# Pacing the loads of the prologue to three in flight, and moving one step of w_in's second slice, in a fused retention + SiLU MLP kernel

## The chip, the cores and the metric

The kernel runs on one core of a Trainium2 chip. A core has a matrix engine (PE; its weight loads are shown apart as PEld), a vector engine (DVE), a scalar engine (ACT), GpSimd (POOL), and SyncE (SP), which here issues nearly all DMA transfers, in the order in which they stand in its queue. Each engine works through its own list in order, and waits on semaphores for the others. The metric is the device time of one execution in microseconds; the median over several executions counts.

## The reference

What is computed is a retention layer, written as a recurrence, whose output is the input of a two-matrix MLP with SiLU:

```
q, k, v: (B=4, H=8, S=768, D=64) float32
state = gamma_h * state + outer(k_t, v_t)          # per batch and head, for t = 0..767
y_t   = scale * (q_t @ state)
x     = y as (B*S = 3072, H*D = 512)
h     = x @ w_in          # w_in  (512, 2048), stored as float64
out   = (h * sigmoid(h)) @ w_out   # w_out (2048, 512), stored as float64
```

## The kernel before

The sequence is cut into 6 chunks of 128 positions; a chunk of one batch is a unit, so there are 24 units, numbered 4 * chunk + batch. For a unit, k, q and v (256 KB each) are loaded; k and q are turned over by PE into PSUM (tiles `kp`, `qp`) and copied out by ACT (`kt`, `qt`); DVE scales k by the decay (line 424); PE forms the scores and the state's increment (`sc`, lines 518 and 528); DVE masks the scores (`am`, line 536) and forms `mid` and `state`; PE forms `y` (line 576), which is split by ACT and DVE into three parts (`xt`). A product of the MLP takes `xt` of a whole chunk (512 rows) and one 128-column slice of w_in, also in three parts (`wi`), and is closed by ACT and DVE (`gk` or `g`).

w_in comes as float64. `load_w(i)` loads a slice as words in three transfers, one of 256 KB (line 193) and two of 128 KB (line 195). The generator `early_slice(i)` turns it into float32 and then splits it; each call `W(i)` runs one step of it. For slice 1, the eighth call copies the high part on ACT (line 126), the ninth and tenth form the two low parts on DVE (line 118); the earlier calls do the conversion (lines 212 to 231).

The first two chunks or so (units 0 to 8, the first steps of unit 9, and the first products of the MLP) are written out by hand, call by call, and for SP, DVE, ACT and POOL the order of the calls is the order of the queues; PE's order is written by hand throughout. In it `T`, or `TK` and `TQ`, turn k and q over, `K` scales k, `SC` forms scores, `A` does DVE's steps on them, `Q` scales q, `YS`, `Y0` and `YB` form y, `X` splits it, `PP` and `PH` are parts of MLP products, `CL` closes one. `load("q", 6)` issues the load of unit 6's q. Calls that only concern different engines can stand in either order without any effect.

All loads of units 0 to 5 and of slices 0 and 1 are issued at the start, one behind the other. Those from `load("k", 6)` on are written among the calls of units 3 to 8, far ahead of their use. In the queue, each transfer also waits on a semaphore of its own lane, of which there are eight used in turn (DMAHW0 to DMAHW7); a transfer that goes into a buffer waits for the buffer's last readers as well.

Of the kernel before, what the change touches and what calls it, by code (L numbers as in the profile page):

```python
# [35 lines left out]
def kernel(  # L36
# [28 lines left out]
    nc = tc.nc  # L65
    B, H, S, D = q.shape
    DM, DF = moe_w_in.shape
    C = 128
# [64 lines left out]
    def split_w(*of):  # L133
        steps = split_steps(*of)
        next(steps)
        yield
        list(steps)
# [15 lines left out]
    early, last = {}, []  # L153

    def load(name, n):
        if n >= len(units):
            return
        c, b = units[n]
        src = {"k": k, "q": q, "v": v}[name]
        if n == 4 * B and name == "k":  # L160
            t = conv.tile([128, H, D], FP32, tag="wl", name=f"kf_{n}")
            nc.sync.dma_start(out=t, in_=src[b, :, ds(c * C, C)].rearrange("h t d -> t h d"))
            kqv[name][n] = t
            return
        if n < EARLY:

            if n not in early:
                early[n] = wpool.tile([128, 3, H, D], FP32, tag=f"w{4 + n}", name=f"kqv_{n}")
            t = early[n][:, "kqv".index(name)]
        else:  # L170
            t = ld.tile([128, H, D], FP32, tag=f"{name}f", name=f"{name}f_{n}",
                        bufs=2 if name == "q" else 3)
        nc.sync.dma_start(out=t, in_=src[b, :, ds(c * C, C)].rearrange("h t d -> t h d"))  # L173
        kqv[name][n] = t

    staged = {}

    def load_w(i):
        if i >= 2 * NF:
            return
        if wide:
            t = stage.tile([128, 2 * DM], U32, tag="wf", name=f"wf_{i}")
            w_in, w_out, n = moe_w_in.bitcast(U32), moe_w_out.bitcast(U32), 256
        else:
            t = stage.tile([128, DM], FP32, tag="wf", name=f"wf_{i}")
            w_in, w_out, n = moe_w_in, moe_w_out, 128
        if i < NF:  # L190
            to = t.rearrange("p (i o f) -> o p i f", o=2, f=n)
            src = w_in[:, ts(i, n)].rearrange("(i o p) f -> o p i f", o=2, p=128)
            last[:] = [nc.sync.dma_start(out=to[0], in_=src[0]).ins]
            for j in range(2):
                nc.sync.dma_start(out=to[1, ts(j, D)], in_=src[1, ts(1 - j, D)])
        else:
            nc.sync.dma_start(out=t, in_=w_out[ts(i - NF, 128), :])
        staged[i] = t
# [35 lines left out]
    def convert_w(i):  # L234

        if patient[0]:
            waiting.append(i + W_AHEAD)
        elif i + W_AHEAD not in staged:
            load_w(i + W_AHEAD)
        out = []  # L240
        steps = convert_steps(i, out)
        for _ in range(6):
            next(steps, None)

        def rounded():
            list(steps)
            return out[0]

        return rounded

    def early_slice(i):

        out = []
        yield from convert_steps(i, out)
        yield
        steps = split_steps(i, out[0], "wi", w_sb, None)
        next(steps)
        yield from steps
# [44 lines left out]
    def begin_w():  # L303

        i = taken[0]
        taken[0] += 1
        split = split_w(i, convert_w(i)(), "wi", w_sb, True)
        next(split)
        half_split.append(split)
# [102 lines left out]
    def hold(done):  # L412

        i = nc.sync.nop().ins
        tc.add_manual_dep(i, done.name, mybir.DependencyInfo(
            mybir.DependencyClass.Sync, mybir.DependencyReason.DATA), reason="hold")
# [276 lines left out]
    def halves(m):  # L693
# [36 lines left out]
        for name in "kqv":  # L730
            for n in (m + 1, m + 2):
                if (n, name) not in apart and EARLY <= n <= LATER and n == (
                        m + 1 if name == "v" or n >= LATER else m + 2):
                    load(name, n)
# [144 lines left out]
    def A(n):  # L879
        next(asteps[n], None)  # L880
# [7 lines left out]
    def TQ(n):  # L888
        next(tsteps[n])
# [20 lines left out]
    def W(i, times=1):  # L910
        if i not in slices:
            slices[i] = early_slice(i)
        for _ in range(times):
            next(slices[i], None)

    def loads(n):
        for name in "kqv":
            load(name, n)
# [39 lines left out]
    def CL(f):  # L958
        next(closing[f], None)

    def KA(n):
        t = kqv["k"][n]
        for h in range(H):
            nc.scalar.activation(out=t[:, h, :], in_=t[:, h, :], func=AF.Copy,
                                 scale=gk[:, units[n][0], h : h + 1])


    load("k", 0)
    load("q", 0)
    load("v", 0)  # L970
    load_w(0)
    load("k", 1)
    load("q", 1)
# [5 lines left out]
    load("q", 3)  # L979
    load("v", 3)  # L980
    load_w(1)
    load("k", 4)
    load("q", 4)
# [83 lines left out]
    X(3)  # L1067
    TQ(4)
    W(1)
    load("k",6)  # L1070
    W(1)
    load_w(2)
# [9 lines left out]
    load("k",9)  # L1082
    PH(0,2,1)
    CL(0)
    W(1)
    load("v",7)
    A(4)
    load("k",8)
# [3 lines left out]
    Q(4)  # L1092
    A(4)
    K(5)
    W(1)
    CL(0)
    YS(4)
# [104 lines left out]
    Q(8)  # L1202
    load("q",11)
    taken[0] = 3
    begin_w()

    early_order.close()
# [9 lines left out]
    last = ([(c, f) for c in range(2) for f in range(NF - 4, NF)] +  # L1217
            [(2, f) for f in range(half, NF)])
# [84 lines left out]
    def apart_cols(t):  # L1303

        return t.rearrange("p (o n) -> p o n", o=2)

    def unwoven(t):

        return t.rearrange("p (n o) -> p o n", o=2)
# [8 lines left out]
    for c in range(NC):  # L1318
# [9 lines left out]
        for f in range(NF):  # L1328
# [4 lines left out]
            t = ready[n]  # L1333
            if f >= early_f:
                continue
            for b in range(B):
                gh, glo, gm = (t[:, i, ts(b, C)] for i in range(3))
                oa, ob = acc[b]
                for o, g, i in (oa, gh, 0), (oa, glo, 1), (ob, gm, 2):
                    nc.tensor.matmul(o, lhsT=g, rhs=woven(wo[f][:, i, :],  # L1340
                                                          (c, b) == (NC - 1, B - 1)),
                                     start=f == 0 and i != 1,
# [4 lines left out]
        if early_f < NF:  # L1347
# [3 lines left out]
                         for x in ("left", "right")]  # L1351
            nc.scalar.activation(out=apart_cols(halves_of[0]),
                                 in_=unwoven(acc[B - 1][0][:, left]), func=AF.Copy,
# [7 lines left out]
        for b, o, parts, cols in ends:  # L1361
            for f in range(early_f, NF):
                for i in parts:
# [3 lines left out]
                                     start=o is last_left and (f, i) == (early_f, 0),  # L1367
                                     stop=f == NF - 1 and i != 0,
                                     skip_group_check=cols != whole)
        for b in range(B):  # L1370
            oa, ob = acc[b]
            if c == NC - 1 and b == B - 1:
# [4 lines left out]
                for i, (x, cols, op) in enumerate(((last_left, left, ALU.add),  # L1377
                                                   (oa, right, ALU.subtract))):
                    nc.vector.scalar_tensor_tensor(
                        out=apart_cols(o[i]), in0=unwoven(x[:, cols]), scalar=ONE_E,  # L1380
# [44 lines left out]
```

## Time and profile before

| | |
|---|---|
| median of 3 executions | 587.9 us (587.0 to 588.2) |
| the profiled execution's own time | 586.36 us |
| its span, first to last instruction | 584.4 us |
| PE busy, share of the span | 576.4 us, 99% |
| DVE, ACT, POOL busy | 399.1, 321.7, 29.4 us |
| granted PE clock | 0.999 |
| DMA, mean over the span | 186 GB/s |

The views give times from the span's start. A row of the timeline has the start, the duration, engine, line, operation, out<-in, shape, how many instructions were merged, and in brackets the engine's idle time ahead of it and what ended that. "issue" stands for idle time in which the engine waited for nothing that the profile shows. SPq rows are SP's issuing of a transfer: the duration is that of the issue, not that of the transfer, whose time from issue to landing stands in the list of DMA issues. PE's ends are modelled, so that a row without idle time can still hide a short one. The 2 us between the span and the execution's own time lie outside of the instructions.

### The profile page before, as it was taken

The page shows a single profiled execution, that of the slowest core. Times are in us where ns is not written, and L with a number is a line of the kernel's source. Part 1 is how long each engine was busy: PE and PEld are TensorE (multiplying, and loading weights), DVE is VectorE, ACT ScalarE, POOL GpSimd, SP SyncE. Part 2 cuts the span into 40 slices and gives each one's busy share as a digit, 9 for nine tenths or more (in the row PEclk, how much of TensorE's full clock was granted, in tenths as well). Part 3 has the DMA queues.
Part 4 walks back from the last instruction along what each step waited for, and adds up shares of the span by engine and source line. Part 5 has one row for each costly group of instructions (what it writes and reads, how often), then busy time and mean ns, then how long its engine had stood idle before and what let it go on. Part 6 is the DMA issues. An engine that isn't in the chain of part 4 may idle for free.

```text
span 584.4 us, 13651 instructions
## 1 busy us (share of the span) xinstructions
PE 576.4 (99%) x5512; PEld 499.9 (86%) x5512; DVE 399.1 (68%) x678; ACT 321.7 (55%) x561; POOL 29.4 (5%) x84
## 2 busy tenths in 40 slices
PE   8999999999999999999999999999999999999997
PEld 6787888888888888888888888888888888888886
DVE  3898998678678876666799994736545563645632
ACT  7657766546356466545566675544544545545311
POOL 3000000100031211210000000000000000000000
PEclk9999999999999999999999999999999999999999
DMA  9998978986489899997589862523524443433301
GB/s 193 215 220 192 218 192 278 267 259 214 145 192 232 234 283 284 255 265 230 171 281 326 288 207 77 195 93 111 178 79 139 144 119 97 165 123 102 115 1 72
DMA packets 144334, 108.89 MB, mean 186 GB/s; under 512 B 101136, under 2 KB 109584, under 8 KB 144272
## 3 DMA queue, kind: packets, MB, share of 16 engines
q1 hardware_dynamic: 144128, 107.90, 66.0%
q8 instruction: 43, 0.70, 0.5%
q14 instruction: 19, 0.16, 0.1%
q10 hardware_dynamic: 144, 0.13, 0.1%
HBM read 66.06 MB, written 36.70 MB: 176 GB/s over the span
## 4 chain that ended last, share of the span: by engine, by line
PE 95%; SPq 2%; DVE 1%; DMA 1%; issue 1%; ACT 0%; DVEq 0%; POOL 0%; POOLq 0%; ACTq 0%
PE ha L757 28%; PE o L1340 21%; PE oa L1340 14%; PE hb L757 14%; PE ob L1340 7%; PE y L576 4%; PE sc L518 2%; PE sc L528 2%; SPq L173 1%; DMA kqv<-in_q_dram 1%; PE ha L928 1%; PE kp L486 1%; PE qp L486 0%; PE o L1364 0%; PE hb L928 0%
## 5 line engine op out<-in xcount | busy, mean ns | idle before, releaser
L757 PE MATMUL ha<-xt,wi 128*128 128x512 f32 x736 | 175.7, 382 | 0.0
L757 PEld LDWEIGHTS ha<-xt,wi 128*128 128x128 f32 x736 | 137.7, 189 | 20.0
L1340 PE MATMUL o<-wo,gs 128*128 128x512 f32 x564 | 137.2, 379 | 0.0
L1340 PEld LDWEIGHTS o<-wo,gs 128*128 128x128 f32 x564 | 106.5, 189 | 15.3 <-DVE o L1389 0.2
L852 DVE TENSOR_TENSOR gs<-gr,gs 128x512 fp32r<-128x512 f32 x96 | 62.0, 684 | 83.0 <-ACT gs L850 83.0
L1340 PE MATMUL oa<-wo,gs 128*128 128x512 f32 x376 | 111.8, 379 | 0.0
L849 ACT ACTIVATE gr<-gr 128x512 f32<-128x512 f32 x96 | 59.7, 629 | 67.8 <-DMA gr<-gd 63.8
L757 PE MATMUL hb<-xt,wi 128*128 128x512 f32 x368 | 94.4, 379 | 0.0
L781 ACT ACTIVATE g<-ha 128x512 f32<-128x512 f32 x87 | 52.1, 599 | 76.5 <-PE ha L757 64.9
L787 DVE SCALAR_TENSOR_TENSOR g<-hb,g 128x512 f32<-128x512 f32 x87 | 59.7, 686 | 40.5 <-ACT g L781 33.6
L1340 PEld LDWEIGHTS oa<-wo,gs 128*128 128x128 f32 x376 | 71.1, 189 | 10.1
L757 PEld LDWEIGHTS hb<-xt,wi 128*128 128x128 f32 x368 | 69.6, 189 | 9.9
L850 ACT ACTIVATE gs<-gr 128x512 fp32r<-128x512 f32 x96 | 53.1, 621 | 38.7 <-PE ob L1340 30.4
L1340 PE MATMUL ob<-wo,gs 128*128 128x512 f32 x188 | 71.3, 379 | 0.0
L853 DVE SCALAR_TENSOR_TENSOR gs<-gs 128x512 fp32r<-128x512 f32 x96 | 61.9, 682 | 0.1
L1340 PEld LDWEIGHTS ob<-wo,gs 128*128 128x128 f32 x188 | 35.5, 189 | 5.1
L212 ACT ACTIVATE ca<-wf 128x512 f32<-128x512 f32 x32 | 27.1, 847 | 15.1 <-DVE cs L225 9.1
L225 DVE SCALAR_TENSOR_TENSOR cs<-ca,cs 128x512 uint32<-128x512 uint32 x32 | 22.1, 690 | 0.8
L536 DVE TENSOR_TENSOR am<-sc,decay 128x512 f32<-128x512 f32 x24 | 16.5, 686 | 8.8 <-PE sc L528 7.7
L576 PE MATMUL y<-qt,mid 64*64 64x64 f32 x376 | 20.0, 220 | 0.9 <-issue 0.9
L657 DVE SCALAR_TENSOR_TENSOR xt<-xt 128x512 fp32r<-128x512 f32 x28 | 19.6, 704 | 0.5
L1389 DVE TENSOR_TENSOR o<-o,o 128x512 f32<-128x512 f32 x10 | 6.6, 687 | 17.8 <-ACT o L1388 17.8
(137 smaller groups left out, 582.9 us busy)
## 6 DMA issues: line engine op xcount, KB each, us to landing
gr<-gd SPq DMA_DIRECT2D x96, 256.0 KB, 2.8
gd<-g SPq DMA_DIRECT2D x87, 256.0 KB, 3.8
wf<-in_moe_w_out_dram SPq DMA_DIRECT2D x16, 512.0 KB, 4.4
out_dram<-o SPq DMA_DIRECT2D x23, 256.0 KB, 2.4
wf<-in_moe_w_in_dram SPq DMA_DIRECT2D x16, 256.0 KB, 4.4
wf<-in_moe_w_in_dram SPq DMA_DIRECT2D x32, 128.0 KB, 4.2
kf<-in_k_dram SPq DMA_DIRECT2D x16, 256.0 KB, 4.6
qf<-in_q_dram SPq DMA_DIRECT2D x16, 256.0 KB, 4.4
```

Source lines behind the costliest of these rows:

```text
L212: top = nc.scalar.activation(out=a.bitcast(FP32), in_=hi.bitcast(FP32), func=AF.Abs, scale=2.0 ** -3).ins
L225: nc.vector.scalar_tensor_tensor(out=s, in0=a, scalar=3, in1=s, op0=ALU.logical_shift_left, op1=ALU.bitwise_xor)
L576: i = nc.tensor.matmul(to[ts(e, D), o, a, :], lhsT=lhsT, rhs=rhs, start=key not in started, stop=True, skip_group_check=True).ins
L657: nc.vector.scalar_tensor_tensor(out=x[2], in0=x[1].bitcast(FP32), scalar=-1.0 / EPS, in1=x[0].bitcast(FP32), op0=ALU.mult, op1=ALU.add)
L757: nc.tensor.matmul(hb if i == 2 else ha, lhsT=w_sb[f][:, i, ts(kk, 128)], rhs=woven(xt[c][:, i, kk, :]), start=kk == 0 and i != 1, stop=kk ...
L781: copied[:] = [nc.scalar.activation(out=to, in_=ha, func=AF.Copy, scale=scale * ONE_E).ins]
L787: taken_out[:] = [nc.vector.scalar_tensor_tensor(out=to, in0=hb, scalar=-scale, in1=to, op0=ALU.mult, op1=ALU.add).ins]
L849: nc.scalar.activation(out=g, in_=g, func=AF.Silu)
L850: nc.scalar.activation(out=t[:, 0, :], in_=g, func=AF.Copy, scale=HALF)
L852: nc.vector.tensor_tensor(out=t[:, 1, :], in0=g, in1=high, op=ALU.subtract)
L853: nc.vector.scalar_tensor_tensor(out=t[:, 2, :], in0=t[:, 1, :].bitcast(FP32), scalar=-1.0 / EPS, in1=high, op0=ALU.mult, op1=ALU.add)
L1340: nc.tensor.matmul(o, lhsT=g, rhs=woven(wo[f][:, i, :], (c, b) == (NC - 1, B - 1)), start=f == 0 and i != 1, stop=f == NF - 1 and i != 0 o ...
```

## The change

From unit 6's k on, up to the end of the part written by hand, each load of k, q, v and of w_in's slices waits until the third load ahead of it has landed: `hold` makes SP wait for that transfer's semaphore. Until then only the lane, eight transfers back, and the buffer were waited for. The stores are not paced, and the loads behind `pace[0] = 0` aren't either; slice 5 of w_in is the first of them. The second part of the change moves the eighth call `W(1)` from ahead of `load("v", 7)` to behind `K(5)`, next to the ninth.

```
+    flying, pace = [], [0]
+
+    def paced(start, **operands):
+        if pace[0] and len(flying) >= pace[0]:
+            hold(flying[-pace[0]])
+        flying.append(start(**operands).ins)
+        return flying[-1]
...
-        nc.sync.dma_start(out=t, in_=src[b, :, ds(c * C, C)].rearrange("h t d -> t h d"))
+        paced(nc.sync.dma_start, out=t, in_=src[b, :, ds(c * C, C)].rearrange("h t d -> t h d"))
...
-            last[:] = [nc.sync.dma_start(out=to[0], in_=src[0]).ins]
+            last[:] = [paced(nc.sync.dma_start, out=to[0], in_=src[0])]
             for j in range(2):
-                nc.sync.dma_start(out=to[1, ts(j, D)], in_=src[1, ts(1 - j, D)])
+                paced(nc.sync.dma_start, out=to[1, ts(j, D)], in_=src[1, ts(1 - j, D)])
...
     W(1)
+    pace[0] = 3
     load("k",6)
...
     CL(0)
-    W(1)
     load("v",7)
...
     K(5)
+    W(1)
     W(1)
     CL(0)
...
     taken[0] = 3
+    pace[0] = 0
     begin_w()
```

`hold`, which stood in the kernel before without a caller:

```
    def hold(done):
        i = nc.sync.nop().ins
        tc.add_manual_dep(i, done.name, mybir.DependencyInfo(
            mybir.DependencyClass.Sync, mybir.DependencyReason.DATA), reason="hold")
```

On SP, the loads from unit 6's k to unit 6's v stood thus before (kqv_6 holds unit 6's k, q and v; wf_2 is slice 2 of w_in; kqv_5's three loads stand just ahead, on lanes 5, 6 and 7):

```order
L173 DMA kqv_6_821<-in_k_dram 128x8x64 [waits DMAHW0_49]
L193 DMA wf_2_823<-in_moe_w_in_dram 128x2x256 [waits DMAHW1_49,DVE_49,Activation_49]
L195 DMA wf_2_823<-in_moe_w_in_dram 64x2x256 [waits DMAHW2_49]
L195 DMA wf_2_823<-in_moe_w_in_dram 64x2x256 [waits DMAHW3_49]
L173 DMA kqv_6_821<-in_q_dram 128x8x64 [waits DMAHW4_49]
L173 DMA kqv_7_828<-in_k_dram 128x8x64 [waits DMAHW5_49]
L173 DMA kqv_6_821<-in_v_dram 128x8x64 [waits DMAHW6_49]
```

and stand thus now (what was lines 173, 193 and 195 is line 181):

```order
L181 DMA kqv_6_821<-in_k_dram 128x8x64 [waits DMAHW5_49,DMAHW0_49]
L181 DMA wf_2_824<-in_moe_w_in_dram 128x2x256 [waits DVE_49,DMAHW1_49,DMAHW6_49,Activation_49]
L181 DMA wf_2_824<-in_moe_w_in_dram 64x2x256 [waits DMAHW7_49,DMAHW2_49]
L181 DMA wf_2_824<-in_moe_w_in_dram 64x2x256 [waits DMAHW0_49,DMAHW3_49]
L181 DMA kqv_6_821<-in_q_dram 128x8x64 [waits DMAHW1_49,DMAHW4_49]
L181 DMA kqv_7_833<-in_k_dram 128x8x64 [waits DMAHW2_49,DMAHW5_49]
L181 DMA kqv_6_821<-in_v_dram 128x8x64 [waits DMAHW3_49,DMAHW6_49]
```

The order is the same; each has one more wait, for the lane three places ahead. The same holds for the 19 loads behind these, up to unit 11's q.

On ACT, around the high part of slice 1 (`wi1`), the list before (kt and qt are copies of k and q turned over, of units 4, 5 and 6):

```order
L487 COPY qt_4_818<-qp_4_802 128x512 [waits PE_49]
L781 ACTIVATE gk_7_880<-ha_0_0_704 128x512 [waits DMAHW6_49,DMAHW5_49,PE_49]
L126 ACTIVATE wi1_882<-cs_1_758 128x512 [waits DVE_49]
L487 COPY kt_5_895<-kp_5_889 128x512 [waits PE_49]
L487 COPY qt_5_903<-qp_5_890 128x512 [waits PE_49]
L487 COPY kt_6_992<-kp_6_986 128x512 [waits PE_49,Activation_49]
```

and now:

```order
L493 COPY qt_4_818<-qp_4_802 128x512 [waits PE_49]
L787 ACTIVATE gk_7_889<-ha_0_0_704 128x512 [waits DMAHW6_49,DMAHW5_49,PE_49]
L493 COPY kt_5_904<-kp_5_898 128x512 [waits PE_49]
L493 COPY qt_5_912<-qp_5_899 128x512 [waits PE_49]
L126 ACTIVATE wi1_918<-cs_1_758 128x512 [waits DVE_49]
L493 COPY kt_6_1004<-kp_6_998 128x512 [waits PE_49,Activation_49]
```

One ACT instruction went behind two copies. DVE's list has the same instructions in the same order as before; the moved call is one of ACT. PE's list too is unchanged, but for a wait on ACT at the first product with slice 1.

## The prediction

> **What bounds the kernel now.** I read the page first, then a table of stretches, PE's waits and its timeline, and last the loads: when they are issued, how long they take, who uses them. The page and the stretches (length; then busy time and instructions of PE, PEld, DVE, ACT, POOL; clock; share of the DMA engines; GB/s):
>
> ```profile
> span 584.4 us, 13651 instructions
> PE 95%; SPq 2%; DVE 1%; DMA 1%; issue 1%; ACT 0%; DVEq 0%; POOL 0%; POOLq 0%; ACTq 0%
> ...
> 26.00:54.00 28.00, 26.66 (x670) 22.53 (x671) 25.39 (x46) 18.12 (x40) 0.36 (x4) 1.00 1.00 216
> 54.00:60.00 6.00, 6.00 (x150) 5.20 (x152) 4.76 (x10) 4.25 (x10) 0.09 (x1) 1.00 0.68 169
> 60.00:300.00 240.00, 240.00 (x2806) 208.59 (x2796) 187.43 (x319) 137.32 (x216) 23.61 (x34) 1.00 0.87 234
> ```
>
> The second row is the chain that ended last: it is PE for 95%. From 60 to 300 us PE is busy in 240.00 of 240.00 us, so whatever makes PE later or earlier by 60 us moves the end by as much. The change acts on 26 to 60 us alone. There PE lacks 28.00 - 26.66 = 1.34 us, DVE is the next with 25.39 of 28, and the DMA engines are full (1.00). What PE waited for there:
>
> ```profile
> PE y L576 <- issue: 0.9, 2, 0.6
> PE sc L518 <- issue: 0.3, 1, 0.3
> PE y L576 <- POOL token L407: 0.3, 1, 0.3
> PE y L576 <- DVE qt L429: 0.2, 1, 0.2
> ```
>
> The reader is to see that no load is among them: before, every paced load landed ahead of its use. (One of the two "issue" waits of the first row, of 0.6 us, began ahead of 26 us.) So the loads can't be made to matter less; they can only stay hidden, or come out. What else is to be had is the rest of these waits, 1.3 us in 26 to 54 us.
>
> **The loads, one by one.** Issues on SP, then the transfers' times from issue to landing, in the order: unit 6's q, its v, the last piece of slice 2, the last of slice 3, and unit 5's k:
>
> ```profile
> 23.07 0.88 SPq L173 DMA_DIRECT2D kqv<-in_k_dram  x1
> ...
> 26.16 0.82 SPq L173 DMA_DIRECT2D kqv<-in_k_dram  x1
> ...
> 29.02 0.61 SPq L195 DMA_DIRECT2D wf<-in_moe_w_in_dram  x1
> 29.67 0.60 SPq L173 DMA_DIRECT2D kqv<-in_q_dram  x1
> ...
> 31.48 2.22 SPq L173 DMA_DIRECT2D kqv<-in_v_dram  x1
> ...
> 47.03 0.60 SPq L195 DMA_DIRECT2D wf<-in_moe_w_in_dram  x1
> ```
>
> ```profile
> kqv<-in_q_dram SPq DMA_DIRECT2D x1, 256.0 KB, 5.5
> kqv<-in_v_dram SPq DMA_DIRECT2D x1, 256.0 KB, 5.6
> wf<-in_moe_w_in_dram SPq DMA_DIRECT2D x1, 128.0 KB, 5.4
> wf<-in_moe_w_in_dram SPq DMA_DIRECT2D x1, 128.0 KB, 5.4
> kqv<-in_k_dram SPq DMA_DIRECT2D x1, 256.0 KB, 4.4
> ```
>
> So they landed at 29.67 + 5.5 = 35.2 (q6), 31.48 + 5.6 = 37.1 (v6), 29.02 + 5.4 = 34.4 (slice 2), 47.03 + 5.4 = 52.4 (slice 3) and 23.07 + 4.4 = 27.5 (k5). Their first uses, on PE and ACT:
>
> ```profile
> 36.40 0.60 PE L486 MATMUL qp<-ident,kqv 128*128 128x128 f32 x4
> 38.81 0.69 PE L518 MATMUL sc<-kqv 64*64 64x64 f32 x32
> 36.21 0.76 ACT L212 ACTIVATE ca<-wf 128x512 f32<-128x512 f32 x1
> 54.78 0.89 ACT L212 ACTIVATE ca<-wf 128x512 f32<-128x512 f32 x1
> ```
>
> The margins are 1.2 us for q6, 1.7 for v6, 1.8 for slice 2 and 2.4 for slice 3. Those of the other paced loads that I looked up are larger.
>
> **The change, part by part.**
>
> *The start of the pacing.* Unit 6's k, issued at 26.16, now waits for unit 5's k, which landed at 27.5: 1.4 us later. This costs nothing, since the engines are full: unit 5's q and v still lie in front of it, and the transfers that it would have waited behind are done meanwhile.
>
> *The pace, 256 KB loads.* In this stretch the engines moved 216 GB/s, which is 262,144 B / 216,000 B per us = 1.21 us for a load. With three in flight a load takes at least the time that it takes with little else on the queue, which a load of q shows that is issued at 166.60:
>
> ```profile
> 166.60 0.40 SPq L173 DMA_DIRECT2D qf<-in_q_dram  x1
> ...
> qf<-in_q_dram SPq DMA_DIRECT2D x1, 256.0 KB, 3.0
> ```
>
> Three in 3.0 us is one in 1.0 us, under 1.21. The engines then remain the limit, the time from issue to landing settles at 3 x 1.21 = 3.6 us instead of 5.5, and the landings come as often as before. Cost 0. The other bound is the shortest time of a load in the full stretch, the 4.4 us of unit 5's k: three in 4.4 us is one in 1.47, 0.26 us later with each load. I take the first, as with three in flight the queue is between the two, and 3.6 follows from the engines' own rate.
>
> *The pace, slices of w_in.* Their three transfers count as three, though they hold 512 KB together, so that 2 x 1.21 = 2.43 us of engine time now fill a turn of at least 3.0 us. That is 0.6 us later after each of the slices 2, 3 and 4. The engines also lose time whenever one of them is held up by something else and the other 15 run out of their three loads; an instruction fetch (below) is 1.25 us on one engine. I estimate 0.3 us per slice for it, a quarter of a fetch, so 0.9 us together. Above, all six transfers at the pace of 4.4 us would be late by 6 x 0.26 = 1.6 us at v6.
>
> *What then is late.* With 0.9 us, q6 lands at 36.1, 0.3 us ahead of its use; v6 at 38.0, 0.8 ahead; slice 3 (two slices' worth, 1.8 us) at 54.2, 0.6 ahead. All stay hidden, by little. What is queued behind the waiting load on SP is loads only, up to 62.88, where the first store stands. After the last paced load, at 53.92, SP issues nothing up to 57.77 anyway, as slice 5 waits for its buffer, and this takes up the lag:
>
> ```profile
> 53.92 0.82 SPq L173 DMA_DIRECT2D qf<-in_q_dram  x1
> 57.77 0.37 SPq L193 DMA_DIRECT2D wf<-in_moe_w_in_dram  x1
> ...
> 62.88 1.03 SPq L631 DMA_DIRECT2D yd<-ys  x1
> ```
>
> Cost 0, and if q6 is late by up to 0.3 us more, PE has some of it to spare: at 38.81 it starts right behind DVE's scaled k.
>
> *The moved step.* ACT and DVE around it:
>
> ```profile
> 30.37 0.63 ACT L126 ACTIVATE wi<-cs 128x512 fp32r<-128x512 f32 x1 [1.24 <-DVE cs L231]
> 30.91 0.57 ACT L487 COPY kt<-kp 128x512 f32<-128x512 f32 x1
> 31.38 0.59 ACT L487 COPY qt<-qp 128x512 f32<-128x512 f32 x1
> 35.25 0.59 ACT L487 COPY kt<-kp 128x512 f32<-128x512 f32 x1 [3.28 <-PE kp L486]
> 32.72 0.68 DVE L118 CUSTOM_DVE_ANT_0 wi<-cs,wi 128x512 fp32r<-128x512 f32 x1
> ```
>
> The list shows that it is an ACT step that goes behind two copies, and DVE's order stays. The copies can start as soon as PE has turned k over, some 0.2 us earlier; PE's waits above name no ACT copy. The high part then comes third, at about 31.8 to 32.4, still ahead of DVE's 32.72, which is where DVE arrives by its own list. ACT was idle for 3.28 us behind it. Cost 0, covered by DVE's queue; without that cover it would be 0.3 to 0.5 us.
>
> *The fetches.* PE's "issue" waits lie inside of runs of small matmuls. Ahead of the first of them, in 29.7 to 31.0 us, the DMA engines carried a transfer of kind "instruction"; then the three waits, the middle one from the chain (start, length):
>
> ```profile
> q8 instruction: 1, 0.02, 6.0%
> ...
> 32.50 0.27 PE L576 MATMUL y<-qt,state 64*64 64x64 f32 x1 [0.31 <-issue]
> ...
> 46.34 0.14 issue
> ...
> 52.39 0.27 PE L518 MATMUL sc<-vf,kf 64*64 64x64 f32 x1 [0.32 <-issue]
> ```
>
> 6.0% of 16 engines in 1.3 us is 1.25 us on one engine, in the middle of the loads' packets. Fewer loads in flight could shorten the fetch; a gain is bounded by the waits, 0.31 + 0.14 + 0.32 = 0.8 us. I take 0.1 us of gain: the engines are as full as before. The Trainium skill (DMA: Bandwidth & Descriptors, Queues, rings and completion order) has each engine take turns between the queues packet by packet, by which the depth of the loads' queue would not matter to a fetch at all, and the sum would have 0 here.
>
> *The sum.* 0 (start) + 0 (256 KB loads) + 0 to 0.3 (slices, as long as hidden) + 0 (moved step) - 0.1 (fetches): +0.1 us on the profiled execution's 586.36. The median of the runs shown is 587.9, 1.5 us above that one, so I forecast 588.0. The Trainium skill (DMA: Bandwidth & Descriptors, Anatomy of one DMA) gives 2.0 us plus bytes over 436 GB/s, 2.6 us for 256 KB. By that estimate the slices would cost less than 0.2 us each, and no margin would come near zero; the row of 3.0 us speaks against so short a time.
>
> **The rivals.**
>
> *Three in flight are too few* (slower). For it: margins of 0.3 to 0.8 us are left by my own count, and the bound of 4.4 us breaks them. Then q6 is late by 35.2 + 4 x 0.26 + 0.9 - 36.4 = 0.7, v6 by 37.1 + 1.6 + 0.9 - 38.8 = 0.8, and slice 3, 18 transfers on, by 52.4 + 18 x 0.26 + 1.8 - 54.8 = 4.1 us, from which PE's own lateness is to be taken. It decides once a load takes more than 3 x 1.21 = 3.6 us with three in flight. Halfway to the bound I get 1.5 us, so 589.5; at the bound 592. Against it: the idle queue's 3.0.
>
> *The fetches get short* (faster). If a fetch no longer shares its engine with loads, all of the three waits go, 0.8 us: 587.1. From 32.50 on, DVE, not PE, sets the next start at 38.81, so that the first of the waits would return there. Against it stands the full share of the engines, and the rule above. The Trainium skill (Runtime: NRT & Kernel Launch, Instruction fetch mechanics) calls the crossing of a 16 KiB block mostly hidden; the rows of 0.31 and 0.32 us differ.
>
> *Nothing happens* because the lanes paced the loads anyway. At most eight were in flight by them; at 5.5 us and 1.21 us a load it was 4 to 5, so three is less. This rival has the time of the forecast and is counted with it.
>
> **How the numbers follow.** Chances: all loads stay hidden 0.62, too few in flight 0.27, short fetches 0.11. Executions before lie between 587.0 and 588.2, so 0.2% (1.2 us) is about what a measurement can tell from no change. The first case is within 0.2% but for scatter (0.54, and 0.04 on each side); the second is slower by more in 0.20 and within in 0.07; the third faster by more in 0.05, within in 0.06. Together: faster 0.09, within 0.67, slower 0.24. The range goes from 586.9 (the fetch case) to 590.0 (the second case somewhat past its halfway value); above it I leave 0.08, below it 0.08.
>
> **What would show it.** In the changed profile: the paced loads at 3.5 to 3.8 us from issue to landing, against 5.5; SP's issues short, its time going into waits on landings; PE's waits without a load among them, and still with "issue"; the ACT copies of unit 5 ahead of the high part; slices landing about 1 and 2 us later. I am wrong if PE's waits from 36 to 59 us name a transfer, ACT's idle time ahead of line 212 does, or if the "issue" waits are gone.

## The result, and the profile after

The changed kernel takes 590.56 us (median of 6 executions, 588.83 to 591.35), the kernel before 588.02 (6 executions, 587.00 to 588.23): a ratio of 1.0047, interval 1.0035 to 1.0060. It is slower by 2.5 us, and 590.56 lies above the forecast of 588.0 and above its range. The profiled execution of the changed kernel took 589.75 us, 3.4 more than that of before.

From the page of the changed kernel, its chain of waits, and from its table of stretches the same three as before (length; busy time and instructions of PE, PEld, DVE, ACT, POOL; clock; share of the DMA engines; GB/s):

```profile
span 587.8 us, 13675 instructions
PE 90%; DMA 7%; SPq 2%; ACT 0%; issue 0%; DVEq 0%; DVE 0%
```

```profile
26.00:54.00 28.00, 24.77 (x644) 20.86 (x646) 25.69 (x46) 16.67 (x34) 0.35 (x4) 1.00 0.78 177
54.00:60.00 6.00, 5.45 (x67) 4.42 (x56) 3.83 (x8) 4.38 (x11) 0.00 (x0) 1.00 0.67 168
60.00:300.00 240.00, 238.96 (x2899) 207.74 (x2900) 185.91 (x317) 136.01 (x216) 23.02 (x35) 1.00 0.89 235
```

In the chain, transfers went from 1% to 7% and PE from 95% to 90%; SP's issuing has 2% in both. From 26 to 54 us the DMA engines are busy for 0.78 of the time and move 177 GB/s, where they were full and moved 216. PE's missing time has grown from 1.34 to 3.23 us there, and past 60 us, where it had none, it lacks 1.04.

PE's waits from 26 to 70 us (engine, tile, line, what was waited for; us in total, times, longest), and behind them the same waits on PE's timeline:

```profile
PE kp L502 <- DMA qf<-in_q_dram: 1.4, 2, 1.0
PE sc L524 <- DMA kqv<-in_v_dram: 1.3, 1, 1.3
PE qp L492 <- DMA kqv<-in_q_dram: 0.7, 1, 0.7
PE sc L524 <- DMA vf<-in_v_dram: 0.5, 1, 0.5
PE y L582 <- issue: 0.3, 1, 0.3
...
PE kp L502 <- DMA kf<-in_k_dram: 0.2, 1, 0.2
```

```profile
37.34 0.63 PE L492 MATMUL qp<-ident,kqv 128*128 128x128 f32 x4 [0.67 <-DMA kqv<-in_q_dram]
...
40.95 0.69 PE L524 MATMUL sc<-kqv 64*64 64x64 f32 x32 [1.26 <-DMA kqv<-in_v_dram]
...
53.38 0.69 PE L524 MATMUL sc<-vf,kf 64*64 64x64 f32 x32 [0.50 <-DMA vf<-in_v_dram]
...
60.44 0.27 PE L502 MATMUL kp<-ident,qf 64*128 64x64 f32 x1 [1.00 <-DMA qf<-in_q_dram]
...
65.91 0.24 PE L502 MATMUL kp<-ident,kf 64*128 64x64 f32 x1 [0.19 <-DMA kf<-in_k_dram]
...
66.87 0.27 PE L502 MATMUL kp<-ident,qf 64*128 64x64 f32 x1 [0.41 <-DMA qf<-in_q_dram]
```

These are unit 6's q and v, unit 8's v, unit 10's q, and unit 11's k and q. The six waits are 0.67 + 1.26 + 0.50 + 1.00 + 0.19 + 0.41 = 4.0 us. Of the three "issue" waits of before, the first is still there with 0.3; those of 0.14 and 0.32 are gone. So 4.0 - 0.46 = 3.5 us, against the 3.4 between the two profiled executions: the loss is PE's waiting for late loads, all of it before 67 us.

ACT came late to slices 2 and 3 as well (line 212 of before is 218 now):

```profile
36.72 0.67 ACT L218 ACTIVATE ca<-wf 128x512 f32<-128x512 f32 x1 [0.29 <-DMA wf<-in_moe_w_in_dram]
...
57.51 0.88 ACT L218 ACTIVATE ca<-wf 128x512 f32<-128x512 f32 x1 [1.27 <-DMA wf<-in_moe_w_in_dram]
```

No wait of PE names ACT or the slices' tiles, so these two cost the kernel nothing directly.

The paced loads: SP's issues for unit 6's k, slice 2, unit 6's v, and units 10's and 11's q, and transfer times from issue to landing, first of unit 6's k and v alone, then medians over the k, q and v loads issued from 36 to 54 us:

```profile
27.80 0.37 SPq L181 DMA_DIRECT2D kqv<-in_k_dram  x1
29.00 4.14 SPq L181 DMA_DIRECT2D wf<-in_moe_w_in_dram  x3
...
36.68 0.37 SPq L181 DMA_DIRECT2D kqv<-in_v_dram  x1
...
56.84 0.37 SPq L181 DMA_DIRECT2D qf<-in_q_dram  x1
...
62.14 0.52 SPq L181 DMA_DIRECT2D qf<-in_q_dram  x1
```

```profile
kqv<-in_k_dram SPq DMA_DIRECT2D x1, 256.0 KB, 4.7
...
kqv<-in_v_dram SPq DMA_DIRECT2D x1, 256.0 KB, 4.1
...
kf<-in_k_dram SPq DMA_DIRECT2D x3, 256.0 KB, 4.4
kqv<-in_v_dram SPq DMA_DIRECT2D x2, 256.0 KB, 3.7
qf<-in_q_dram SPq DMA_DIRECT2D x2, 256.0 KB, 4.7
vf<-in_v_dram SPq DMA_DIRECT2D x2, 256.0 KB, 4.9
```

A load of 256 KB with three in flight takes about 4.4 us, not 3.6 (single ones 3.2 to 5.4); SP's issues are short, as its time goes into the new waits; and the last paced load, unit 11's q, is issued at 62.14, where it stood at 53.92.

The moved step went where the order said:

```profile
30.84 0.58 ACT L493 COPY kt<-kp 128x512 f32<-128x512 f32 x1 [1.61 <-PE kp L492]
31.32 0.59 ACT L493 COPY qt<-qp 128x512 f32<-128x512 f32 x1
31.80 0.64 ACT L126 ACTIVATE wi<-cs 128x512 fp32r<-128x512 f32 x1
```

DVE's low part follows at 32.82, against 32.72 before.

### The profile page after: what moved, and what is told of

The parts are those of the page before. It is cut to its first block, busy times and chain, and to the rows that moved or that the text cites. A ratio compares the mean times of both kernels' runs of the same rounds, so it can differ in the third digit from the quotient of the medians.

```text
span 587.8 us, 13675 instructions
## 1 busy us (share of the span) xinstructions
PE 575.3 (98%) x5512; PEld 499.0 (85%) x5512; DVE 400.0 (68%) x678; ACT 322.2 (55%) x561; POOL 28.5 (5%) x84
## 4 chain that ended last, share of the span: by engine, by line
PE 90%; DMA 7%; SPq 2%; ACT 0%; issue 0%; DVEq 0%; DVE 0%
PE ha L763 27%; PE o L1348 21%; PE oa L1348 14%; PE hb L763 13%; PE ob L1348 7%; PE y L582 4%; DMA qf<-in_q_dram 2%; SPq L181 2%; DMA wf<-in_moe_w_in_dram 1%; PE sc L524 1%; PE sc L534 1%; DMA kf<-in_k_dram 1%; DMA kqv<-in_q_dram 1%; DMA vf<-in_v_dram 1%; DMA kqv<-in_k_dram 1%; PE o L1372 0%
```

## The experiments

Every kernel is compared with the kernel before on the same chip. In most of them the lateness of loads is what tells. It is worked out thus, from rows as above: a load's landing (issue plus time to landing) less the landing of unit 5's k, one of the last three loads that nothing paces in any of them, and the one that unit 6's k waits for in the changed kernel, and this less the same for the kernel before. In the changed kernel, for instance, unit 6's k landed at 27.80 + 4.7 = 32.5, 4.8 behind unit 5's; before, 3.4 behind it; it is 1.4 late.

| late by, us | unit 6's k | 6's q | 9's v | 10's q | 11's q |
|---|---|---|---|---|---|
| the changed kernel | 1.4 | 1.9* | 5.4 | 6.2* | 8.0 |
| e2, pace alone | 1.3 | 2.7 | 4.6 | 5.1 | 7.2 |
| e3, four in flight | -0.1 | -0.6 | 3.2 | 3.8 | 6.0 |
| e4, a slice counts as one | 1.0 | 1.7 | 3.4 | 3.7 | 2.7 |
| e5, slices alone wait | -0.3 | 0.0 | 1.3 | 1.8 | 2.9 |
| e6, two in flight | 1.0 | 4.2 | 10.8 | 13.8 | 17.9 |
| e10, four, a slice as one | -0.3 | -0.5 | 0.4 | 0.2 | 0.2 |

(* the landing is missing in the records; it is taken from the start of PE's first matmul behind the wait.) Each row is one execution, and the scatter between executions is not small: in e1, which paces nothing, unit 9's v came 1.3 and unit 10's q 1.0 us later than in the profiled execution of before.

### e1: the moved step alone

```
-    pace[0] = 3
+    pace[0] = 0
     load("k",6)
```

> The eighth step of slice 1 is moved as in the change, and no load is paced. Theory L (late loads: with three in flight a load takes 4 to 5 us from issue to landing, and PE waits for it): same as before within 0.1%, PE's waits as before. Rival M (the moved ACT step delays DVE's low part and what follows): the whole +2.5 us is here, about 590.5, and DVE's row at line 118 starts later than 32.7 us.

586.41 against 586.61 us, ratio 1.0003 (0.9989 to 1.0017). The moved step costs nothing that can be told. PE waits for no load in e1. DVE's low part starts at 33.01, later than 32.7, but the high part is done at 32.6 (ACT) and the low part stands right behind DVE's scaling of k (32.40, 0.68 us long), so it is DVE's own queue that holds it. PE's waits with "issue" come to 1.8 us in this profile, more than before, so they are not the same from one execution to the next.

### e2: the pace alone

The eighth `W(1)` stands where it stood before:

```
     CL(0)
+    W(1)
     load("v",7)
...
     K(5)
     W(1)
-    W(1)
```

> The loads are paced as in the change, and the ACT step stays where it was. Theory L: the same as the whole change, ratio to before 1.0047 with its interval of about 0.001, and PE waits for unit 6's q, unit 6's v, unit 8's v and unit 10's q by name, 3 to 4 us together. Rival M: the time of before.

589.11 against 586.61 us, ratio 1.0046 (1.0030 to 1.0063): 2.5 us, so the whole loss comes with the pace. The stretch of 26 to 54 us and PE's waits up to 80 us of this kernel:

```profile
26.00:54.00 28.00, 25.79 (x670) 21.92 (x669) 25.96 (x47) 17.52 (x38) 0.35 (x4) 1.00 0.77 178
```

```profile
PE qp L492 <- DMA kqv<-in_q_dram: 1.4, 1, 1.4
PE kp L502 <- DMA qf<-in_q_dram: 1.0, 2, 0.8
PE kp L502 <- DMA kf<-in_k_dram: 0.6, 1, 0.6
```

Again 1.4 + 1.0 + 0.6 = 3.0 us of waits for loads, though spread otherwise: the longest is for unit 6's q, and no v is named. From unit 6's v at 39.60 to units 7's v, 9's q and 9's v, each three loads later, the landings stood at 44.16, 48.49 and 52.88: 4.4 us to a turn of three, from a landing to that of the load which waited for it. In the kernel before, the same four landed at 37.04, 41.41, 44.50 and 48.61, 3.9 to three loads, since the engines were not full all the time there either. The kernel before and e2 from 38 to 54 us:

```profile
38.00:54.00 16.00, 15.15 (x428) 12.61 (x422) 14.36 (x26) 11.03 (x28) 0.27 (x3) 1.00 0.91 207
```

```profile
38.00:54.00 16.00, 15.63 (x435) 13.19 (x434) 14.38 (x25) 10.92 (x26) 0.26 (x3) 1.00 0.76 177
```

So the pace costs (4.43 - 3.86) / 3 = 0.19 us for each 256 KB load here.

### e3: four in flight

```
-    pace[0] = 3
+    pace[0] = 4
```

> The change with four loads in flight instead of three, all else as in it. Theory L: if the turn is what counts, a load of about 4.5 us gives one landing in 1.13 us, which is the engines' own rate of 1.21, so the lateness is nearly gone: PE's waits on loads under 0.5 us together, ratio 1.000 to 1.001. Rival S (the extra wait on each load costs by itself, in SP's queue, whatever the depth): still more than 1.5 us above before.

587.06 against 586.61 us, ratio 1.0013 (1.0002 to 1.0024). Only unit 11's q was waited for, 1.1 us, which is more than the 0.5 expected. As four in flight take most of the loss away, the extra wait on each load is not what costs (rival S). Unit 6's k now waits for unit 4's v and goes out at 26.16, as before, and nothing is late up to unit 6's q; from there the lateness grows to 3.2 at unit 9's v and 6.0 at the end. It stayed below the margins until the very last load.

### e4: three in flight, a slice counts as one

The first piece waits, the last one is counted:

```
             for j in range(2):
-                paced(nc.sync.dma_start, out=to[1, ts(j, D)], in_=src[1, ts(1 - j, D)])
+                flying[-1] = nc.sync.dma_start(out=to[1, ts(j, D)], in_=src[1, ts(1 - j, D)]).ins
```

> Three in flight, but a slice of w_in counts as one load: only its first piece waits, and only its last piece is counted. If the slices' three-for-one counting is the main cost (the prediction put 0.6 us on each of three slices and 0 on the loads of 256 KB), PE's waits on loads fall from 4.0 us to under 1, ratio under 1.002. If it is the turn of the 256 KB loads, well over half of the loss stays, ratio 1.003 or more.

586.22 against 586.61 us, ratio 0.9995 (0.9984 to 1.0005). The loss is gone, though not all of the waits: those for loads come to 1.3 us, where under 1 was expected. PE's waits up to 80 us:

```profile
PE kp L502 <- DMA qf<-in_q_dram: 0.7, 1, 0.7
PE qp L492 <- DMA kqv<-in_q_dram: 0.6, 1, 0.6
PE sc L524 <- DVE kqv L430: 0.5, 1, 0.5
PE y L582 <- issue: 0.3, 1, 0.3
```

The wait for unit 6's q is as long as in the changed kernel, 0.6 against 0.7, so it is there without the counting too, but the way to it is another. SP's issue of unit 6's q, in the changed kernel and in e4:

```profile
33.27 0.53 SPq L181 DMA_DIRECT2D kqv<-in_q_dram  x1
```

```profile
31.74 0.54 SPq L181 DMA_DIRECT2D kqv<-in_q_dram  x1
```

In the changed kernel it goes out when slice 2's first piece has landed (33.2), and that piece was not late itself. In e4 it goes out 1.5 us earlier, takes 5.4 us behind unit 6's k and the three pieces of slice 2, and lands at 37.1, no earlier. The waits for v and for unit 11 are gone. At unit 11's q the lateness falls from 8.0 or 7.2 to 2.7 us, so three transfers instead of one cost (7.2 - 2.7) / 3 = 1.5 to (8.0 - 2.7) / 3 = 1.8 us for each of the three slices. What counting does to the engines is seen from 32 to 34 us, behind slice 2. The kernel before, the changed one, and e4 (the share adds up the times of packets, and can exceed 1):

```profile
32.00:34.00 2.00, 1.69 (x92) 1.52 (x96) 2.00 (x5) 0.00 (x0) 0.09 (x1) 1.00 1.32 220
```

```profile
32.00:34.00 2.00, 1.67 (x85) 1.49 (x88) 2.00 (x4) 0.44 (x1) 0.09 (x1) 1.00 0.15 46
```

```profile
32.00:34.00 2.00, 1.51 (x84) 1.38 (x88) 2.00 (x4) 0.44 (x1) 0.09 (x1) 1.00 0.74 199
```

In the changed kernel the three in flight there were unit 6's k and slice 2's first two pieces, with landings at 32.5, 33.2 and 33.6: so close together that the engines ran nearly empty (0.15) until the three loads issued behind them were under way.

### e5: only the slices wait

The transfers of k, q and v are counted, but wait for nothing:

```
-        paced(nc.sync.dma_start, out=t, in_=src[b, :, ds(c * C, C)].rearrange("h t d -> t h d"))
+        flying.append(nc.sync.dma_start(out=t, in_=src[b, :, ds(c * C, C)].rearrange("h t d -> t h d")).ins)
```

> Only the pieces of w_in's slices wait for the third load ahead; k, q and v are counted but go out without the wait. If the pieces' own waits were the cost (theory P), most of the 2.5 us is here. If the cost arises because the loads behind a slice spend their turns of three on its small pieces (theory T, by the run in which a slice counts as one), SP catches up behind each slice, q6 lands within 1 us of before, and the ratio is under 1.0015.

587.92 against 586.46 us, ratio 1.0017 (1.0005 to 1.0029), just beyond the expected 1.0015. In its profile no load is waited for; there are two longer waits with "issue" instead (0.82 at 42.30, 0.66 at 47.21), as in the profile of e1, whose median shows no loss. So the loss needs both kinds of waits: with those of the slices alone there is about a third of it (0.17% of 0.46%), and as no load is waited for, the profile does not show whether late loads cause even that; with those of k, q and v and one to a slice (e4) there is none that can be told.

### e6: two in flight

```
-    pace[0] = 3
+    pace[0] = 2
```

> The change with two in flight. Theory T: a turn, from one landing to that of the load which waited for it, was 4.4 us for k, q and v in the changed kernel and about 3.2 for pieces. With two in flight I expect some 4.0 us a turn for two, 2.0 per load, so that unit 11's q, 25 loads behind unit 6's k, lands near 32 + 25 x 1.9 = 79 us where PE wants it near 63: 12 to 18 us above before, 599 to 605. If the extra wait costs by itself and the depth doesn't matter, the time is that of the change, about 2.5 us above before.

601.24 (two executions) against 586.46 us, ratio 1.0243 (1.0214 to 1.0273), as expected. The longest waits:

```profile
39.73 0.63 PE L492 MATMUL qp<-ident,kqv 128*128 128x128 f32 x4 [2.99 <-DMA kqv<-in_q_dram]
...
57.41 0.90 PE L524 MATMUL sc<-vf,kf 64*64 64x64 f32 x32 [1.99 <-DMA vf<-in_v_dram]
...
68.03 0.36 PE L502 MATMUL kp<-ident,qf 64*128 64x64 f32 x1 [2.95 <-DMA qf<-in_q_dram]
...
76.77 0.27 PE L502 MATMUL kp<-ident,qf 64*128 64x64 f32 x1 [1.50 <-DMA qf<-in_q_dram]
```

Late loads, then, scale with the pace: 17.9 us at the end with two in flight, 7.2 to 8.0 with three, 6.0 with four. PE's waits named here are 9.4 us, less than the 14.8 of the medians and the 16.35 of the profiled execution (602.71); by the estimate in the last section the clock makes up the rest.

### e7 and e8: unit 6's q ahead of slice 2

As e4's two remaining waits are for q, e7 moves unit 6's q ahead of slice 2 and unit 10's v behind unit 10's q, on top of e4; e8 does the same in the kernel before, unpaced:

```
     load("k",6)
     W(1)
-    load_w(2)
     load("q",6)
+    load_w(2)
...
     load_w(3)
-    load("v",10)
...
     load("q",10)
+    load("v",10)
     load_w(4)
```

> Three in flight with a slice counted as one, and two loads in another order: unit 6's q ahead of slice 2, unit 10's v behind its q. In the run without this order PE waited 0.59 and 0.68 us for just these two q. Theory T (what is left of the pacing's cost is the lateness of these two): both waits go, 0.5 to 1.2 us less than that run, ratio to before 0.998 to 0.999. If PE's fetches and DVE take back what the loads give, the ratio stays at 0.9995.

> The kernel before, without any pacing, and with the two loads in that same order: the control for the run above. No load was late before, so all theories expect the time of before within 0.1%. If this one is as fast as the paced one with the same order, pacing has nothing to do with the gain.

587.17 us (1.0007, 0.9990 to 1.0024) and 587.39 (1.0010, 0.9997 to 1.0023), against 586.46: neither gains, so the expectation for e7 is missed. In e7 the waits for q went, and one of 1.3 us for DVE's scaled k of unit 6 took their place (the other in the row is unit 5's, as in e4), since that stands on DVE behind steps of slice 2, whose last piece now lands later. PE's wait and DVE's row in e7:

```profile
PE sc L524 <- DVE kqv L430: 1.8, 2, 1.3
```

```profile
37.92 0.49 DVE L221 TENSOR_SCALAR cs<-wf 128x512 uint32<-128x512 uint32 x1 [0.87 <-DMA wf<-in_moe_w_in_dram]
```

### e9: two in flight and more instruction fetches

With two in flight some loads took 3.0 us and others 4.3. To see whether an instruction fetch holds up the longer ones, e9 adds 512 small matmuls on a tile of zeros to e6, 128 ahead of the turning of q in each of the units 6 to 9; their results are overwritten.

```
                 t = tp[i].rearrange("p (a t) -> p a t", a=HP)
+                narrow(tp[i], 128 if i == 1 and n in (6, 7, 8, 9) else 0)
                 for a in range(HP):
```

> The kernel with two loads in flight, and ahead of PE's turning over of q of units 6, 7, 8 and 9 stand 128 more small matmuls each (256 instructions with their weight loads, as many as one fetch brings), into a bank that is written anew right behind them; the output stays as it is. The loads don't depend on them. Theory F (an instruction fetch holds one DMA engine for about 1 us and, with so few loads in flight, the landing of a load with it): with two in flight, loads without a fetch took 2.9 to 3.2 us and those with one 3.8 to 5.3; with three to four more fetches ahead of it, unit 9's v lands 2 to 4 us later, counted from unit 5's k, than the 31.9 us of that run. If fetches don't matter to loads, 31.9 us within 0.5. The time of the whole tells nothing here, as PE has 512 more matmuls to do.

603.54 against 586.51 us, ratio 1.0290 (1.0265 to 1.0314); the added matmuls cover most of the waits, so this time says little. From unit 5's k to unit 9's v, where e6 had six fetches, e9 had eight instead of the nine or ten expected, and v landed 31.8 us after k, in e6 31.9. Two more fetches made nothing late. That fetches lengthen the loads is not confirmed, on a small difference.

### e10: four in flight, a slice counts as one

e3's and e4's edits together.

> A slice counts as one load, and four instead of three are in flight. Theory T: no load is late at all, the times from issue to landing are 4.5 to 5.5 us as before, and the ratio to before is 1.000 within 0.001. If fewer loads in flight had a gain of their own (shorter fetches), it would show here as 0.999 or less.

586.47 against 586.51 us, ratio 1.0004 (0.9993 to 1.0016). No load is late by more than 0.4 us at the five places of the table, PE waits for none, and there is no gain either. Of the versions run, none is faster than the kernel before.

## Why the prediction was wrong, point by point

- **The moved step**: right. e1 shows 0, and in the changed kernel DVE's low part starts at 32.82 against 32.72.
- **What bounds the kernel**: right. The loss appears up to 67 us and is handed through to the end (3.5 us of waits, 3.4 between the profiled executions).
- **The pace, 256 KB loads: this step failed.** It took 1.21 us to a load and so 3.6 to a turn of three, from the engines' rate when they were full, put the cost at 0, and left 4.4 as the other bound. Measured are 4.4 to a turn (e2), and in the changed kernel 177 GB/s and engines busy for 0.78. The engines are no longer the limit; the loads' time in a queue of three is. The row of 3.0 us, of a load with little else on the queue, was the wrong neighbour, that of 4.4 us in the full stretch the right one. The count at that bound, given as a rival, is close: for unit 6's q 4 x 0.26 + 0.9 = 1.9 us (measured 1.9 and 2.7), for unit 9's v, 15 transfers on, 15 x 0.26 + 0.9 = 4.8 (5.4 and 4.6). Part of that is luck, as errors offset each other. 0.26 a load is too much: the 1.00 of the engines was a mean, they were at 0.91 from 38 us on, and e2 gives 0.19; e4, in which a slice costs one wait, has 3.4 - 1.0 = 2.4 us at unit 9's v beyond the first load's lag, 0.18 to each of 13 waits. A slice's 0.9 is too little, and the first load's lag was left out.
- **The start of the pacing: failed, by 1.0 to 1.4 us.** The wait of unit 6's k for unit 5's was costed at nothing because of full engines. Unit 6's k landed 1.4 us late in the changed kernel, 1.3 in e2 and 1.0 in e4, while in e3 and e10, where it goes out as early as before, it is not late. In e4 this lag goes with the wait for unit 6's q, which is 1.7 late there with a margin of 1.2: in e5, where unit 6's k is not held but slice 2's pieces are, that q is on time (0.0), and in e10 too (-0.5). In the changed kernel that q waited for slice 2's first piece, and the share of this lag in its 1.9 us is not shown.
- **Slices of w_in: the mechanism was right, the size was not.** 0.9 us to a slice was the estimate, 1.5 to 1.8 is what e4 against e2 and the changed kernel gives. The step counted engine time against a turn of 3.0 us; with 4.4 the same subtraction gives 4.4 - 2.43 = 2.0. This is the largest term: of the 7.2 us by which unit 11's q is late in e2, 4.5 go when a slice counts as one, and with them the loss.
- **What then is late: failed, by these sizes.** It compared the smallest margins (1.2 to 2.4 us) with a lag that grows with every load. Unit 10's q was needed at 57.9 and landed at 54.0, unit 11's q at 63.4 and 58.6: margins of 3.9 and 4.7, larger, but further along. With 0.9 us to a slice and nothing else they would have been late by 1.8 and 2.7, and still hidden; at the bound of 4.4 by 20 x 0.26 + 1.8 = 7.0 and 25 x 0.26 + 2.7 = 9.2, and not. Measured are 5.1 to 6.2 and 7.2 to 8.0. The pause of SP from 53.92 to 57.77 stands behind unit 11's q; it could take up the lag for slice 5, and did nothing for the loads that were late. The load that the rival named there, slice 3, landed 2.6 us behind the 54.8 of its use before (57.4; the rival had 4.1), but only ACT waited for it.
- **The fetches**: no gain shown. The wait of 0.31 at 32.5 is still 0.3 with fewer loads in flight. The two later ones are missing in the changed kernel, but e10, where they are missing too and whose loads are on time, is not faster either. That no "issue" waits remain was named as a sign against the forecast; it turned out to say nothing by itself.
- **The signs** named the failure correctly: PE's waits from 36 to 59 us name transfers (unit 6's q and v, unit 8's v), ACT's idle time ahead of its line 212 does too, and the paced loads stand at 4.4 us and not at 3.5 to 3.8.
- The rival *three in flight are too few* was the right one, at its bound. That its 592 lies near the 590.6 is in part luck: it is the 4.1 us of slice 3, for which PE did not wait, while PE waited 4.0 us for six other loads, four of which the rival did not name, and 0.46 us of other waits went.

The Trainium skill (DMA: Bandwidth & Descriptors, Anatomy of one DMA) gives 2.6 us for 256 KB by its formula, which is fitted to transfers issued by GpSimd; the loads here, issued by SP with three in flight, took 3.7 to 4.9 by the medians above, and the measurement decides. By that estimate a queue of three would have kept the engines full, which it did not.

What stays open is why a load takes 4.4 us with three in flight when the engines are idle for a fifth of the time. Two things can be read. First, a transfer moves nothing right after its issue. In the changed kernel slice 2's last piece is issued at 32.55; what the engines moved from 32 to 36 us, in steps of 0.1 us:

```profile
GB/s 113 92 92 72 41 92 92 51 31 20 10 0 0 0 0 0 0 0 164 41 10 51 133 154 220 169 97 108 118 164 251 241 264 282 279 287 243 220 210 154
```

Nothing moves from 33.1 to 33.8, and the 164 is a single instruction fetch of 16 KB, so some 1.3 us lie between the start of that issue and its first bytes. Second, in e2 the landings come in threes about 1 us apart with 2.5 us between (43.12, 44.16, 45.06; 47.54, 48.49, 49.39). A bunch that lands together is reissued together, and the engines drain in between. That fits, but no run here broke the bunches up, and e9 does not support the fetches as a cause.

## What to carry to other kernels

Before limiting transfers in flight, count the lag along the whole row of paced loads up to the last, not at the smallest margin alone: it grows with each load by the turn over the depth less the time between landings without the limit (here 4.43 / 3 - 3.86 / 3), the first wait adds its own, and small transfers that are counted as full ones add a good part of a turn's share each (here two more to a slice, 1.5 to 1.8 us together, against a share of 1.5 each). For the turn take the time of a transfer in the same traffic, not that of a lone one. Here a depth of three or four with a slice's pieces counted together cost nothing that can be told, with pieces counted singly four cost 0.1%, three 0.5%, and two 2.4%.

## What the runs showed of the hardware that was not expected

In the kernel with two in flight (e6) the granted clock fell after PE's waits. Its stretches right after the waits of 2.99, 1.99, 2.95 and 1.50 us:

```profile
40.00:44.00 4.00, 4.00 (x100) 3.30 (x102) 1.29 (x2) 2.12 (x4) 0.09 (x1) 0.59 0.63 143
...
57.40:60.00 2.60, 2.59 (x66) 2.38 (x67) 0.69 (x1) 0.91 (x4) 0.00 (x0) 0.57 0.75 199
...
68.00:72.00 4.00, 3.97 (x137) 3.79 (x137) 1.48 (x4) 1.20 (x4) 0.09 (x1) 0.57 0.37 111
...
76.80:80.00 3.20, 3.20 (x61) 2.69 (x62) 2.79 (x5) 1.20 (x4) 0.09 (x1) 0.72 1.23 218
```

The clock (the figure ahead of the last two) is 0.57 to 0.59 after the longer three and 0.72 after the last, with PE busy. An estimate of what that cost is the length of a stretch times what the clock lacks: (1 - 0.59) x 4 = 1.6 us after the first. Over these four and the stretches from 60 to 64 us (0.85) and 80 to 84 us (0.79) it comes to 6.8 us; with the 9.4 us of the waits that is 16.2, and the profiled execution took 16.35 us more than that of before. Waits of up to 1.37 us in the changed kernel and in e2 left the clock at 1.00. What decides between 1.37 and 1.50 us is not shown. The Trainium skill (TensorE: Matmul & The Clock Gate, Why this matters for your kernels) warns of idle gaps of more than about 3 us between bursts of matmuls; here the clock fell after gaps of 1.99 and 1.50 us already.

The engines can also be far from full with transfers waiting to be issued: 0.15 busy from 32 to 34 us in the changed kernel, 0.16 in e2.
